# Sinkhorn attention into a hypermixer: another written order, mask products ahead of the first loads, projection weights loaded in fp32

## The chip, the cores and the metric

The kernel runs on one core of a Trainium2 chip. The metric is device time in microseconds of one execution; the median of three runs is shown, and one further execution was recorded by the hardware profiler. The engines are PE (TensorE, the matrix products), ACT (ScalarE), DVE (VectorE), POOL (GpSimd) and SP (SyncE, here a DMA queue). In this kernel PE's results go to PSUM, which it uses as one tile of eight banks of 512 fp32 values per partition, and ACT and DVE copy them out. The trace shows each engine taking its instructions in the written order.

## The reference

Four batches, eight heads, 768 positions, head size 64, eight blocks of 96 positions. A Sinkhorn matrix P of 8 x 8 per head sorts the blocks of k and v; each block of q attends to its sorted block; the eight heads laid side by side (512 columns) then go through a token mixer and an output projection.

```python
P = sort_net
for _ in range(5):
    P = P - np.max(P, axis=-1, keepdims=True)
    P = np.exp(P)
    P = P / (np.sum(P, axis=-1, keepdims=True) + 1e-09)
    P = P / (np.sum(P, axis=-2, keepdims=True) + 1e-09)
k_sorted = np.einsum('bhij,bhjcd->bhicd', P, k_b)
v_sorted = np.einsum('bhij,bhjcd->bhicd', P, v_b)
scores = scale * np.matmul(q_b, k_sb.transpose(0, 1, 2, 4, 3))   # within a block
attn = softmax(scores)
x = np.matmul(attn, v_sb)                  # heads side by side: (4, 768, 512)
wq = x @ w_q;  wk = x @ w_k                # 512 -> 64
W_tok = np.einsum('bsd,btd->bst', wq, wk) / np.sqrt(64)
out = np.maximum(np.einsum('bst,btd->bsd', W_tok, x), 0.0) @ w_out
```

The mixer is computed as wq (wk^T x), so that no 768 x 768 matrix appears.

## The kernel before

The whole program is unrolled, and one string, `ORDER`, gives the order of every unit of work. An item such as `K02:6` is unit K of batch 0, part 2, in PSUM bank 6; capital letters are PE units, small letters the copies that empty the bank, with the engine behind the colon (`k02:D:6`: DVE, bank 6). `l` items are loads, issued on POOL and converting fp32 to bf16 on the way (`lk2` is k of batch 2); R, d and s are DMAs on SP. Since every engine takes its items in this order, an item that waits holds up everything behind it on its engine.

The units, in the order in which a batch needs them:

- a, c: the exponentials (ACT) and the row and column sums (DVE) of the five Sinkhorn rounds, for all 32 heads at once. In `a02` (`u_a`, n = 2) ACT's exponential is followed by eight PE products of the identity that build the mask `m_p`, and by ACT's copy of it. i00 makes the identity `idb` on POOL, i03 sets padding.
- Z: products on a zero tile `fil`, which compute nothing that is used. `Z019` is 19 of them.
- B, u, n: eight PE products spread the matrix (`PbT`, the transposed last result of c05); u copies it to `PTR`; n multiplies it with the mask into `M`, the sorting matrix, two heads at a time on DVE for batch 0, four heads on POOL for the others. M has two buffers.
- Q turns q by transposes, K sorts and turns k in one product with M, V sorts v (b > 0). For batch 0, Y and F sort v by way of a turned copy.
- S, e: scores and ACT's exponential. P, r, x: products with the sorted v, reciprocals and scaling on DVE, to `X`. R brings the sorted v across partitions by DMA, N touches it on POOL.
- T, J, W, G, H: T turns X into `XT`; J gives both projections, `qkT`, from `XT` and the weights `wqk`; d copies its q half to other partitions; W turns the k half back by four 128-column transposes per unit, of which w copies columns 64 to 127 to `wk`; G multiplies wk with X; H mixes and applies the relu.
- O, o, s: the output product of 128 rows by 512 columns in four steps, the copy to `ot`, and the store.

Most PE instructions are recorded at line 147, the helper `mm`, and most copies at lines 151 (ACT) and 153 (DVE), the helper `copy`; groups are told apart by their tiles. The POOL queue, before, runs

```
i00 lq0 i03 lv0 lk0 lq1 n11 lv1 lk1 lq2 n10 n20 lk2 lp n21 lv2 lk3 n31 n30 lq3 lv3 lo N35 N15 N25
```

where `lp` loads the two projection weights and `lo` the output weights. After the last batch POOL checks the reciprocals (lines 442 to 448).

Of the kernel before, what the change touches and what calls it, by code (L numbers as in the profile page):

```python
# [16 lines left out]
ORDER = """
i02:D c00:D a01:A i00:G lq0 Z019:0 Q01:0 Q00:1 c01:D a02:A c02:D a03:A i03:G c03:D a04:A c04:D
Q03:2 a05:A c05:D Z010:3 B00:3 n01:D:3 u00:A:3 lv0 Z02:4 Y01:4 n02:D:3 lk0 n03:D:3 n00:D:3 Y03:6
y01:A:4 lq1 Q02:3 y03:D:6 q01:A:0 Y00:4 y00:A:4 q00:A:1 F01:0 q03:D:2 q02:D:3 Z03:6 K02:6 f01:D:0  # L20
K03:4 Y02:2 k02:D:6 K00:0 K01:6 n11:G lv1 k03:D:4 k01:A:6 y02:D:2 Z01:4 S05:4 e05:A:4 F03:6 k00:D:0
S04:2 S02:4 F02:7 S00:0 f03:D:6 e02:A:4 Q10:6 Q11:4 F00:5 f02:D:7 e04:A:2 e00:A:0 q10:D:6 lk1 S01:2
Q12:6 q11:D:4 f00:D:5 Q13:7 lq2 P03:0 q12:D:6 e01:A:2 n10:G S06:4 e06:A:4 V12:2 q13:D:7 r03:D:0
v12:A:2 V11:6 x03:D:0 S03:4 P04:0 r04:D:0 x04:D:0 v11:A:6 e03:A:4 P00:2 V10:6 K13:0 v10:A:6 r00:D:2
n20:G K10:4 lk2 x00:D:2 k10:A:4 lp K11:2 K12:6 k13:D:0 n21:G k12:D:6 S15:0 P01:4 r01:D:4 k11:A:2
S16:2 e16:A:2 P02:6 S12:2 x01:D:4 e15:A:0 Q21:4 r02:D:6 R14:S R15:S Q20:5 e12:A:2 R13:S R10:S R12:S
x02:D:6 S10:0 S13:2 e10:A:0 q20:D:5 T00:6 T02:7 t02:D:7 e13:A:2 t00:D:6 q21:D:4 S11:0 e11:A:0 T03:5
T01:7 S14:2 e14:A:2 t03:D:5 Q23:6 K20:0 lv2 K21:4 lk3 R11:S k20:A:0 q23:D:6 K23:2 k21:D:4 Q22:6
t01:A:7 K22:0 q22:D:6 n31:G P12:4 k23:A:2 J01:7 k22:A:0 j01:A:7 r12:D:4 x12:D:4 P11:2 J00:6 S20:0
n30:G P10:4 r11:D:2 j00:A:6 S26:6 d01:S e20:A:0 x11:D:2 r10:D:4 W00:2 x10:D:4 e26:A:6 W01:3 lq3  # L30
V22:0 P13:6 w01:A:3 V21:3 w00:D:2 T11:2 r13:D:6 T10:5 v22:A:0 R25:S V20:0 x13:D:6 t10:D:5 v20:D:0
S22:6 v21:A:3 S24:3 t11:D:2 G00:5 d00:S e22:A:6 e24:A:3 G01:5 K32:6 R23:S g00:D:5 P14:0 K31:2 K33:4
k32:A:6 k31:A:2 r14:D:0 T12:6 lv3 x14:D:0 S21:0 T13:7 H02:2 e21:A:0 h02:A:2 k33:D:4 R20:S t12:D:6
H00:4 R24:S K30:0 t13:D:7 Q32:7 R22:S Q31:6 Q33:2 Q30:3 h00:D:4 k30:A:0 q33:D:2 S25:4 S23:0 R21:S
q30:D:3 q32:A:7 e23:A:0 lo q31:D:6 J11:2 J10:3 e25:A:4 S34:6 H01:0 e34:A:6 j11:D:2 V31:4 j10:D:3
P23:2 W10:6 h01:D:0 v31:A:4 r23:D:2 W11:7 w10:D:6 V32:0 w11:A:7 P22:4 x23:D:2 r22:D:4 v32:A:0 d11:S
V30:6 P21:2 v30:A:6 O02:0 O03:1 x22:D:4 P24:4 r21:D:2 P20:6 x21:D:2 o03:A:1 r24:D:4 O00:3 R31:S
T21:1 t21:A:1 G10:2 x24:D:4 o00:A:3 r20:D:6 R34:S o02:D:0 x20:D:6 G11:2 S36:4 S30:0 R30:S s01:S
S32:6 R35:S T20:3 e36:A:4 e30:A:0 O04:4 t20:D:3 g10:D:2 d10:S T22:5 e32:A:6 S33:0 o04:D:4 R33:S
R32:S t22:A:5 S31:2 H10:6 T23:4 h10:D:6 O01:5 t23:D:4 e31:A:2 e33:A:0 O05:2 H12:6 o01:A:5 H11:3  # L40
o05:A:2 h12:D:6 S35:0 s00:S J20:5 j20:A:5 J21:2 P31:6 O14:5 h11:A:3 e35:A:0 r31:D:6 s02:S x31:D:6
j21:A:2 O12:4 o12:A:4 P34:0 P32:6 O11:2 r34:D:0 d21:S O10:4 r32:D:6 o11:A:2 x32:D:6 P30:6 W21:2
o14:A:5 x34:D:0 P33:0 o10:D:4 O15:5 r30:D:6 O13:4 W20:3 w21:A:2 T31:2 x30:D:6 o15:D:5 T30:5 w20:D:3
s10:S r33:D:0 o13:A:4 G20:4 d20:S t30:A:5 x33:D:0 G21:4 T32:3 T33:0 t31:D:2 g20:A:4 H22:6 H21:4
t33:A:0 H20:1 N35:G h21:A:4 h20:A:1 t32:D:3 J30:3 J31:0 j31:A:0 O22:4 s11:S s12:S j30:D:3 d30:D
W30:5 O20:3 W31:0 O23:1 w31:A:0 o23:A:1 w30:D:5 o20:D:3 G30:5 G31:5 h22:D:6 d31:D g30:D:5 N15:G
O21:3 H30:0 N25:G o21:A:3 o22:D:4 s21:S H32:6 O24:5 h30:D:0 O25:4 h32:A:6 o24:A:5 H31:2 s20:S
o25:A:4 O31:7 s22:S h31:D:2 O35:6 O33:2 O30:3 o31:A:7 O34:7 o35:D:6 O32:6 o30:D:3 o33:A:2 s31:S
s35:S s33:S o34:A:7 s30:S s34:S o32:A:6 s32:S
# [4 lines left out]
def kernel(  # L54
# [107 lines left out]
    def u_a(b, n, e, bank):  # L162
        nc.scalar.activation(Pv, Pv, ACT.Exp)  # L163
        if n == 2:
            for j in range(NB):
                mm(PS[:, 7, 0:SP], idb, idb[:, j * SP:(j + 1) * SP], start=(j == 0), stop=(j == NB - 1))
            nc.scalar.copy(m_p, PS[:, 7, 0:SP])
# [483 lines left out]
```

## Time and profile before

| What | Value |
|---|---|
| Median of three runs | 109.87 us (109.6 to 111.01) |
| Profiled execution, its own time | 110.02 us |
| Its span, first to last instruction | 107.8 us |
| Mean granted TensorE clock | 0.984 |
| PE busy | 93.8 us (87%), 1499 matmuls |
| DVE busy | 74.1 us (69%) |
| ACT busy | 65.9 us (61%) |
| POOL busy | 26.5 us (25%) |
| Share of PE in the chain that ended last | 60% |
| Bytes moved by DMA | 19.34 MB, mean 179 GB/s |

The span is what the profile covers; the rest of the execution's own time, 2.2 us, lies around it. Busy shares are means over stages that differ, so the time line and windows of a few microseconds say more than the table. A matmul's recorded duration includes its way through the array, which overlaps the next one's: 35 products on `fil` of 512 columns average 475 ns each in the groups, while warm ones start 216 ns apart. PE's busy share is therefore no measure of how full it is.

### The profile page before, as it was taken

The numbers are of one execution on the slowest core, as the hardware profiler recorded it, in microseconds if no ns is written. First come the engines' busy times: TensorE is split into PE (matmuls) and PEld (weight loads), VectorE is DVE, ScalarE is ACT, GpSimd is POOL, SyncE is SP. The second block draws the span as 40 slices with busy tenths as digits, with TensorE's granted clock in tenths as the row PEclk, the third lists the DMA queues.
The fourth block names the chain that finished last, engine by engine and source line by source line (L and its number), as shares of the span: only waits on it lengthen the run. The fifth ranks groups of instructions, "written<-read, shape, count | busy, mean of one in ns | idle before, by whom it ended". The sixth has DMA issues, their size and how long they took to land.

```text
span 107.8 us, 3505 instructions
## 1 busy us (share of the span) xinstructions
PE 93.8 (87%) x1499; PEld 64.1 (59%) x1499; DVE 74.1 (69%) x146; ACT 65.9 (61%) x95; POOL 26.5 (25%) x45
## 2 busy tenths in 40 slices
PE   5997717989998895998989599999999999999960
PEld 2335315767887784868877378676556685553420
DVE  2630765888979986696977589957756984585420
ACT  4102106527979886987878949289695269347440
POOL 7930006959920990000000000000100047000000
PEclk9999996699999999999999999999999999999999
DMA  0899999999999999999999810375270365009784
GB/s 3 89 200 204 204 203 205 115 199 203 205 206 204 231 235 225 204 204 208 205 231 250 198 29 0 104 249 166 88 299 26 146 228 234 3 3 383 298 324 163
DMA packets 19359, 19.34 MB, mean 179 GB/s; under 512 B 1936, under 2 KB 17424, under 8 KB 19344
## 3 DMA queue, kind: packets, MB, share of 16 engines
q0 software_dynamic: 14064, 10.09, 62.8%
q1 hardware_dynamic: 5280, 9.03, 24.0%
q8 instruction: 11, 0.18, 0.6%
q14 instruction: 4, 0.03, 0.1%
HBM read 20.19 MB, written 6.29 MB: 246 GB/s over the span
## 4 chain that ended last, share of the span: by engine, by line
PE 60%; DMA 12%; ACT 10%; DVE 8%; issue 5%; SPq 1%; POOL 0%; POOLq 0%; ACTq 0%
PE ps L147 60%; DMA Qn<-in_q_dram 7%; DMA qD<-qkT 5%; ACT E L321 5%; ACT Vs L151 3%; DVE KT L153 2%; DVE M L240 1%; DVE X L350 1%; ACT KT L151 1%; DVE tmp L182 1%; ACT Pm L163 1%; DVE Pm L179 1%; DVE tmp L177 1%; DVE tmp L178 1%; DVE tmp L183 1%
## 5 line engine op out<-in xcount | busy, mean ns | idle before, releaser
L321 ACT ACTIVATE E<-ps 96x960 bf16<-96x960 f32 (+1 forms) x28 | 23.7, 898 | 4.2 <-PE ps L147 2.2
L147 PE MATMUL ps<-wo,mixT 128*128 128x512 bf16 x96 | 22.9, 379 | 0.0
L350 DVE TENSOR_TENSOR X<-ps,Rall 96x896 bf16<-96x896 f32 (+1 forms) x20 | 20.0, 1004 | 0.6
L151 ACT COPY ot<-ps 128x512 f32<-128x512 f32 x16 | 9.3, 589 | 9.6 <-PE ps L147 9.5
L147 PEld LDWEIGHTS <-mixT 128*128 128x128 bf16 x96 | 8.6, 97 | 9.0 <-issue 0.6
L147 PE MATMUL ps<-fil 128*128 128x512 bf16 x35 | 11.2, 475 | 1.6 <-DVE fil L195 1.2
L240 POOL TENSOR_TENSOR M<-PTR,m_p 128x512 bf16<-128x512 bf16 x6 | 7.9, 1318 | 16.8 <-ACT PTR L151 10.9
L151 ACT CAST KT<-ps 128x768 bf16<-128x768 f32 x11 | 8.6, 808 | 5.1 <-PE ps L147 4.6
L147 PE MATMUL ps<-VT,E 96*128 96x65 bf16 x256 | 10.8, 193 | 0.0
L412 DVE TENSOR_SCALAR mixT<-ps 128x1024 bf16<-128x1024 f32 x7 | 8.6, 1224 | 3.1 <-PE ps L147 3.1
L147 PEld LDWEIGHTS <-KT 64*128 64x128 bf16 (+1 forms) x288 | 8.6, 98 | 3.5 <-issue 1.9
L147 PEld LDWEIGHTS <-E 96*128 96x128 bf16 x256 | 9.7, 97 | 1.6
L153 DVE CAST KT<-ps 128x768 bf16<-128x768 f32 x9 | 8.3, 953 | 3.0 <-PE ps L147 2.8
L147 PE MATMUL ps<-QT,KT 64*128 64x96 bf16 x256 | 9.3, 204 | 0.2 <-ACT E L321 0.2
L307 POOL COPY gate<-VT 6x1 bf16<-6x1 bf16 x3 | 0.5, 177 | 35.3 <-DMA VT<-Vs 35.2
L147 PE MATMUL ps<-M,Kn 128*64 128x128 bf16 x192 | 7.5, 221 | 1.5 <-ACT E L321 1.1
L147 PE MATMUL ps<-idb,Qn 128*64 128x128 bf16 x192 | 7.4, 226 | 1.1 <-DMA Qn<-in_q_dram 0.8
L151 ACT CAST Vs<-ps 128x1024 bf16<-128x1024 f32 x8 | 7.8, 1014 | 0.2
L147 PEld LDWEIGHTS <-Kn 128*64 128x64 bf16 x192 | 6.0, 109 | 3.0 <-issue 2.8
L147 PEld LDWEIGHTS <-fil 128*128 128x128 bf16 x35 | 3.9, 119 | 6.5 <-issue 3.6
L147 PE MATMUL ps<-XT,wqk 128*128 128x384 bf16 x32 | 6.2, 327 | 1.3 <-issue 1.3
L147 PEld LDWEIGHTS <-Qn 128*64 128x64 bf16 x192 | 6.2, 114 | 1.9 <-DMA Qn<-in_q_dram 1.3
(78 smaller groups left out, 136.5 us busy)
## 6 DMA issues: line engine op xcount, KB each, us to landing
out_dram<-ot SPq DMA_DIRECT2D x9, 512.0 KB, 3.2
...
```

The lines of the kernel that those rows point to most:

```text
L147: nc.tensor.matmul(o, w, x, is_transpose=t, start=start, stop=stop, skip_group_check=True)
L151: nc.scalar.copy(o, i)
L153: nc.vector.tensor_copy(o, i)
L163: nc.scalar.activation(Pv, Pv, ACT.Exp)
L177: nc.vector.reduce_sum(tmp, Pv, axis=AX.X)
L178: nc.vector.reciprocal(tmp, tmp)
L179: nc.vector.tensor_mul(Pv, Pv, rows(tmp))
L182: nc.vector.reduce_sum(tmp, (Pm if n == 1 else Pv).rearrange("p i j -> p j i"), axis=AX.X)
L240: ENG[e].tensor_tensor(out=M[b % 2][:, h0:h0 + hn], in0=src.unsqueeze(2).to_broadcast([P, hn, SP, NB]), in1=m_p.unsqueeze(1).unsqueeze(3). ...
L321: nc.scalar.activation(E[b % 2][:, n, 0:2 * w * BLK].rearrange("p (t a c) -> p a t c", a=2, c=BLK), PS[0:BLK, bank:bank + 2, 0:w * BLK].re ...
L350: nc.vector.tensor_mul(xo.rearrange("p (a t d) -> p a t d", a=2, d=D), avps(bank, w)[:, :, :, 0:D], Rall[:, b, n, :, 0:w].unsqueeze(3).to_ ...
L412: nc.vector.tensor_relu(o, i)
```

## The change

Five things change.

- A new PE unit `A00` holds the eight mask products. It stands first in PE's order; `a02` only copies the result. `lq0` goes ahead of `i00`, and the memsets of `i03` behind `n11`.
- The loads `lp` are gone. SP loads both projection weights at the start, unconverted, four rows (1 KB) per partition, into a part of the output tiles `ot`. Unit z00 casts and interleaves them on ACT, U00 transposes, z01 reorders columns on ACT, U01 transposes back, and z02 writes `wqk` on DVE. (The branch under `SPQ` is off.)
- W takes the k half by products with 64 columns of the identity, in fp32 in PSUM; two units share a bank, and for batches 0 to 2 one copy w empties both.
- For the last batch the output rows 4 and 5 are computed and copied in two halves of 256 columns (`O34` and `O314`, `O35` and `O315`).
- The whole order is another one. Batch 0 sorts k before v. POOL's queue is now

```
lq0 i00 lk0 lv0 lv1 n11 i03 n10 lk1 lq1 n20 lv2 lq2 n21 lq3 lk2 lv3 n30 n31 lk3 N15 lo N25 N35
```

```diff
@@ -13,40 +13,41 @@
 ACT = mybir.ActivationFunctionType
 
 NMIX = 2
+SPQ = False
 
 ORDER = """
-i02:D c00:D a01:A i00:G lq0 Z019:0 Q01:0 Q00:1 c01:D a02:A c02:D a03:A i03:G c03:D a04:A c04:D
-Q03:2 a05:A c05:D Z010:3 B00:3 n01:D:3 u00:A:3 lv0 Z02:4 Y01:4 n02:D:3 lk0 n03:D:3 n00:D:3 Y03:6
-y01:A:4 lq1 Q02:3 y03:D:6 q01:A:0 Y00:4 y00:A:4 q00:A:1 F01:0 q03:D:2 q02:D:3 Z03:6 K02:6 f01:D:0
-K03:4 Y02:2 k02:D:6 K00:0 K01:6 n11:G lv1 k03:D:4 k01:A:6 y02:D:2 Z01:4 S05:4 e05:A:4 F03:6 k00:D:0
-S04:2 S02:4 F02:7 S00:0 f03:D:6 e02:A:4 Q10:6 Q11:4 F00:5 f02:D:7 e04:A:2 e00:A:0 q10:D:6 lk1 S01:2
-Q12:6 q11:D:4 f00:D:5 Q13:7 lq2 P03:0 q12:D:6 e01:A:2 n10:G S06:4 e06:A:4 V12:2 q13:D:7 r03:D:0
...
-O21:3 H30:0 N25:G o21:A:3 o22:D:4 s21:S H32:6 O24:5 h30:D:0 O25:4 h32:A:6 o24:A:5 H31:2 s20:S
-o25:A:4 O31:7 s22:S h31:D:2 O35:6 O33:2 O30:3 o31:A:7 O34:7 o35:D:6 O32:6 o30:D:3 o33:A:2 s31:S
-s35:S s33:S o34:A:7 s30:S s34:S o32:A:6 s32:S
+i02:D c00:D a01:A lq0 i00:G c01:D A00:0 a02:A:0 Z020:0 Q00:0 Q02:1 c02:D a03:A c03:D a04:A c04:D
+z00:A a05:A c05:D q00:A:0 lk0 U00:2 Z09:0 B00:0 n03:D:0 Q01:3 q02:A:1 q01:A:3 n02:D:0 Q03:1 n00:D:0
+z01:A:2 u00:D:0 Z02:4 K00:4 n01:D:0 lv0 k00:A:4 K03:6 K01:2 k01:D:2 q03:A:1 K02:4 lv1 k02:D:4 Z01:0
+S02:0 Y03:2 Y02:4 k03:A:6 n11:G e02:A:0 y02:A:4 Y01:6 y03:D:2 S04:0 e04:A:0 Y00:2 F02:4 y01:D:6
+S05:5 S03:0 i03:G y00:D:2 f02:A:4 n10:G F03:7 e03:A:0 F01:2 S00:3 lk1 V12:0 f03:D:7 F00:7 f01:D:2
+v12:D:0 e05:A:5 e00:A:3 S06:5 f00:D:7 S01:2 P02:0 e06:A:5 e01:A:2 lq1 P04:4 V10:6 K12:2 v10:A:6
+r04:D:4 r02:D:0 x02:D:0 K10:0 x04:D:4 k12:A:2 K11:6 n20:G P03:4 r03:D:4 k11:A:6 P01:2 lv2 V11:6
+k10:A:0 Z01:0 Q13:0 x03:D:4 Q11:1 v11:A:6 r01:D:2 Q10:4 R15:S x01:D:2 R14:S q10:A:4 q11:D:1 P00:5
+q13:D:0 r00:D:5 S12:2 R10:S T01:4 K13:0 e12:A:2 k13:A:0 x00:D:5 Q12:7 S11:2 lq2 U01:5 z02:D:5 n21:G
+R11:S q12:D:7 R13:S V20:0 t01:D:4 T03:6 t03:D:6 lq3 e11:A:2 R12:S v20:A:0 S10:2 S14:4 e10:A:2 S16:0
+e14:A:4 V22:6 T02:2 T00:3 v22:D:6 t02:A:2 P10:4 S15:6 t00:D:3 P11:2 e16:A:0 r10:D:4 x10:D:4 e15:A:6
+r11:D:2 J00:0 lk2 j00:A:0 P13:6 S13:4 x11:D:2 J01:0 Q21:3 r13:D:6 R25:S T10:2 e13:A:4 j01:A:0 lv3
+P14:4 x13:D:6 q21:A:3 r14:D:4 d00:S t10:A:2 n30:G R21:S P12:0 W00:3 V21:6 W01:3 d01:S x14:D:4
+r12:D:0 Q22:2 x12:D:0 Q20:4 v21:A:6 R24:S Q33:5 T11:6 T12:7 n31:G R23:S q20:D:4 q22:A:2 w00:D:3
+T13:4 t11:A:6 q33:D:5 K20:0 K23:2 t13:D:4 K21:5 G00:4 R20:S G01:4 t12:D:7 lk3 Q23:7 k23:A:2 k21:A:5
+R22:S k20:D:0 K22:2 k22:D:2 S21:0 S22:5 g00:A:4 e21:A:0 J10:4 q23:D:7 H00:2 e22:A:5 V31:0 j10:D:4
+h00:D:2 J11:7 v31:A:0 j11:D:7 d11:S V32:4 S26:2 e26:A:2 S23:0 S24:6 e23:A:0 Q32:2 Q31:3 e24:A:6
+v32:D:4 R34:S K31:4 q31:D:3 q32:D:2 K32:0 k31:A:4 K33:6 k32:D:0 H01:2 V30:4 k33:A:6 h01:D:2 P22:0
+W10:6 r22:D:0 v30:A:4 N15:G W11:6 Q30:7 w10:A:6 x22:D:0 S25:2 lo R31:S q30:D:7 e25:A:2 H02:4 O02:6
+P24:0 h02:A:4 R32:S K30:2 r24:D:0 G10:7 k30:A:2 R35:S G11:7 x24:D:0 S20:4 g10:A:7 S34:0 e20:A:4
+R33:S P21:2 d10:S O00:7 P23:4 o02:D:6 r21:D:2 e34:A:0 S32:0 R30:S x21:D:2 S33:2 e32:A:0 o00:D:7
+r23:D:4 O01:6 e33:A:2 T21:7 P20:0 x23:D:4 S36:4 t21:D:7 r20:D:0 S30:2 o01:A:6 e36:A:4 x20:D:0 O03:7
+T23:4 S31:5 o03:D:7 H10:0 T20:7 h10:D:0 e30:A:2 e31:A:5 O05:3 P32:5 P30:0 t20:D:7 T22:7 t23:D:4
+r32:D:5 o05:A:3 r30:D:0 P31:2 O10:4 t22:A:7 x32:D:5 N25:G s01:S x30:D:0 O04:5 S35:6 H12:0 o10:A:4
+r31:D:2 e35:A:6 o04:D:5 J20:4 O11:5 s02:S h12:A:0 x31:D:2 P33:6 o11:D:5 J21:0 j20:D:4 P34:2 O15:1
+o15:A:1 j21:D:0 r33:D:6 W20:0 W21:0 w20:A:0 r34:D:2 T31:4 T30:5 x33:D:6 t31:A:4 O14:1 d21:S t30:A:5
+x34:D:2 T33:0 T32:2 o14:D:1 t32:D:2 H11:6 t33:D:0 G20:5 G21:5 J31:4 d20:S J30:0 s10:S g20:A:5
+h11:D:6 s00:S j31:D:4 d31:D j30:A:0 H20:1 H22:5 H21:3 h20:A:1 h21:D:3 O12:7 W31:0 W30:1 O20:2 O21:3
+O13:4 w31:D:0 h22:A:5 o13:A:4 s12:S o20:A:2 o21:D:3 d30:D O23:0 o12:A:7 w30:D:1 s11:S O22:1 o22:D:1
+G30:2 s20:S G31:2 O25:7 g30:A:2 H31:5 N35:G o23:A:0 O24:0 h31:A:5 H30:3 o24:D:0 H32:1 o25:A:7 O32:5
+h30:A:3 s21:S o32:A:5 O33:0 O31:3 h32:A:1 s22:S s32:S o33:D:0 O30:4 O35:0 o31:A:3 s33:S o30:A:4
+O315:1 s31:S o35:A:0 o315:A:1 O314:4 O34:0 o314:D:4 o34:A:0 s30:S s35:S s34:S
 """
 
 
@@ -107,7 +108,7 @@
 
     NIN = 3
     Qn, Kn, Vn = (tiles(n, NIN, [P, H, R6, D]) for n in ("Qn", "Kn", "Vn"))
-    wqk = sb.tile([P, PT, 2, DH], BF16, name="wqk")
+    wqk = sb.tile([P, PT, 2 * DH], BF16, name="wqk")
     wo = sb.tile([P, PT, DM], BF16, name="wo")
     QT = tiles("QT", 2, [P, NP, R6, P])
     KT = tiles("KT", 2, [P, NP, S + PAD])
@@ -123,6 +124,16 @@
     mixT = tiles("mixT", NMIX, [P, 2, 2, R6, P])
     NOT = 4
     ot = tiles("ot", NOT, [P, 2, DM], FP32)
+    if SPQ:
+
+        q32 = XT[0].rearrange("p t s -> p (t s)").bitcast(FP32).rearrange("p (h r d) -> p h r d", r=R6, d=D)
+        nc.sync.dma_start(out=q32.rearrange("p h r d -> p h (r d)"),
+                          in_=q[0, 0:H // 2].rearrange("h (p r) d -> p h (r d)", p=P))
+
+    w32 = ot[0][:, 0, :].rearrange("p (s x) -> p s x", s=2)
+    w16, wT = (ot[1].rearrange("p a n -> p (a n)").bitcast(BF16)[:, n * DM:(n + 1) * DM] for n in range(2))
+    for s, w in enumerate((moe_w_q, moe_w_k)):
+        nc.sync.dma_start(out=w32[:, s], in_=w.rearrange("(p u) d -> p (u d)", p=P))
     M = tiles("M", 2, [P, H, SP, NB])
     Rall = keep.tile([BLK, B, NG, 2, AG // 2], FP32, name="Rall")
     PTR = sb.tile([P, NB, BH], BF16, name="PTR")
@@ -162,12 +173,14 @@
     def u_a(b, n, e, bank):
         nc.scalar.activation(Pv, Pv, ACT.Exp)
         if n == 2:
-            for j in range(NB):
-                mm(PS[:, 7, 0:SP], idb, idb[:, j * SP:(j + 1) * SP], start=(j == 0), stop=(j == NB - 1))
-            nc.scalar.copy(m_p, PS[:, 7, 0:SP])
+            nc.scalar.copy(m_p, PS[:, bank, 0:SP])
         elif n == 3:
             nc.scalar.copy(Lx.rearrange("p a j s -> p (a j) s"),
                            idb[0:BH, 0:BH].unsqueeze(2).to_broadcast([BH, BH, SP]))
+
+    def u_A(b, n, bank):
+        for j in range(NB):
+            mm(PS[:, bank, 0:SP], idb, idb[:, j * SP:(j + 1) * SP], start=(j == 0), stop=(j == NB - 1))
 
     def u_c(b, n, e, bank):
         if n == 0:
@@ -207,10 +220,7 @@
             nc.gpsimd.memset(Rall[:, :, NG - 1, :, (NU - AG * (NG - 1)) // 2:AG // 2], 1.0)
 
     def u_l(b, n, e, bank):
-        if n == "p":
-            for s, w in enumerate((moe_w_q, moe_w_k)):
-                nc.gpsimd.dma_start(out=wqk[:, :, s, :], in_=w.rearrange("(t p) d -> p t d", p=P))
-        elif n == "o":
+        if n == "o":
             nc.gpsimd.dma_start(out=wo, in_=moe_w_out.rearrange("(t p) d -> p t d", p=P))
         else:
             t, src = {"q": (Qn, q), "k": (Kn, k), "v": (Vn, v)}[n[0]]
@@ -305,6 +315,23 @@
     def u_N(b, n, e, bank):
 
         nc.gpsimd.tensor_copy(gate[0:R6, :], VT[b % 2][0:R6, NB - 1, H - 1, 0:1])
+
+
+
+    def u_U(b, n, bank):
+        for t in range(PT):
+            mm(bf(bank)[:, t * P:(t + 1) * P], (w16, wT)[n][:, t * P:(t + 1) * P], idb, t=True)
+
+    def u_z(b, n, e, bank):
+        if b == 1:
+            copy(e, Qn[0][:, 2 * n:2 * n + 2], q32[:, 2 * n:2 * n + 2])
+        elif n == 0:
+            copy(e, w16.rearrange("p (u s d) -> p s u d", u=PT, s=2),
+                 w32.rearrange("p s (u d) -> p s u d", u=PT))
+        elif n == 1:
+            copy(e, wT.rearrange("x (p u) -> x p u", u=PT), bf(bank)[:, 0:DM].rearrange("x (u p) -> x p u", u=PT))
+        else:
+            copy(e, wqk.rearrange("p t d -> p (t d)"), bf(bank)[:, 0:DM])
 
 
     def u_S(b, n, bank):
@@ -361,7 +388,7 @@
 
     def u_J(b, n, bank):
         for pt in range(PT):
-            mm(PS[:, bank, 0:S // 2], wqk[:, pt].rearrange("p a d -> p (a d)"),
+            mm(PS[:, bank, 0:S // 2], wqk[:, pt, :],
                XT[b % 2][:, pt, n * 384:(n + 1) * 384], start=(pt == 0), stop=(pt == PT - 1))
 
     def u_j(b, n, e, bank):
@@ -375,13 +402,12 @@
             copy(e, o, i)
 
     def u_W(b, n, bank):
-        for ii in range(4):
-            i = 4 * n + ii
-            mm(bf(bank)[0:BLK, ii * P:(ii + 1) * P], qkT[b % 2][:, i * BLK:(i + 1) * BLK], idb, t=True)
+        for i in range(4 * n, 4 * n + 4):
+            mm(PS[0:BLK, bank, i * DH:(i + 1) * DH], qkT[b % 2][:, i * BLK:(i + 1) * BLK], idb[:, DH:P])
 
     def u_w(b, n, e, bank):
-        copy(e, wk[b % 2][:, 4 * n:4 * n + 4, :],
-             bf(bank)[0:BLK, 0:4 * P].rearrange("p (i x) -> p i x", x=P)[:, :, DH:P])
+        i0, i1 = (4 * n, 4 * n + 4) if b == B - 1 else (0, NB)
+        copy(e, wk[b % 2][:, i0:i1, :].rearrange("p i x -> p (i x)"), PS[0:BLK, bank, i0 * DH:i1 * DH])
 
     def u_G(b, n, bank):
         for i in range(4 * n, 4 * n + 4):
@@ -411,16 +437,23 @@
         else:
             nc.vector.tensor_relu(o, i)
 
+    def osplit(b, n):
+
+        r, m = n % 10, n // 10
+        return (r, slice(m * DM // 2, (m + 1) * DM // 2)) if b == B - 1 and r >= R6 - 2 else (r, slice(0, DM))
+
     def u_O(b, n, bank):
+        r, c = osplit(b, n)
         for t in range(PT):
-            mm(PS[:, bank, :], mixT[b % NMIX][:, t // 2, t % 2, n, :], wo[:, t, :],
+            mm(PS[:, bank, c], mixT[b % NMIX][:, t // 2, t % 2, r, :], wo[:, t, c],
                start=(t == 0), stop=(t == PT - 1))
 
     def oslot(b, n):
         return ot[(b * 3 + n // 2) % NOT]
 
     def u_o(b, n, e, bank):
-        copy(e, oslot(b, n)[:, n % 2, :], PS[:, bank, :])
+        r, c = osplit(b, n)
+        copy(e, oslot(b, r)[:, r % 2, c], PS[:, bank, c])
 
     def u_s(b, n, e, bank):
         od = out[b].rearrange("(p r) e -> p r e", r=R6)
```

More of the change, by code (lines that the diff above doesn't have):

```diff
@@ L23 @@
-Q12:6 q11:D:4 f00:D:5 Q13:7 lq2 P03:0 q12:D:6 e01:A:2 n10:G S06:4 e06:A:4 V12:2 q13:D:7 r03:D:0
[L24 to L46, printed above, removed]
```

## The prediction

> **What bounds the kernel now.** I read the page's slices first (PE busy, granted clock, DMA share), then the chain of work that ended last, in order of time, then the list of waits, then busy time by windows.
>
> ```profile
> PE   5997717989998895998989599999999999999960
> PEclk9999996699999999999999999999999999999999
> DMA  0899999999999999999999810375270365009784
> ```
>
> Each column is 2.7 us, counted from 0. PE is full from slice 23 on; DMA is full from slice 2 to 21, the loads of q, k, v. The clock dips in slices 6 and 7.
>
> ```profile
> 1.46 7.53 DMA Qn<-in_q_dram
> ...
> 9.03 1.17 PE ps L147 x32
> 10.19 0.02 issue
> 10.22 0.17 ACT m_p L167
> 10.39 0.16 ACT Pm L163
> ...
> 15.56 0.24 DVE PbT L186
> 15.80 0.04 issue
> 15.84 0.36 PE ps L147 x8
> ...
> 61.62 42.61 PE ps L147 x511
> 104.24 0.02 issue
> 104.26 0.59 ACT ot L151
> ```
>
> ```profile
> ACT m_p L167 <- PE ps L147: 5.3, 1, 5.3
> PE ps L147 <- DVE PbT L186: 2.9, 1, 2.9
> ```
>
> ```profile
> 17.90:25.00 7.10, 6.71 (x126) 5.43 (x125) 5.85 (x9) 3.56 (x6) 5.93 (x7) 0.82 1.18 168
> 65.00:70.00 5.00, 5.00 (x81) 3.57 (x79) 4.76 (x10) 3.00 (x5) 0.00 (x0) 1.00 0.21 55
> ```
>
> The waits give us in total, times and the longest; the windows give their length, the busy time of PE, weight loads, DVE, ACT and POOL, the granted clock, the DMA share and GB/s. Three stages follow. **Front, to 16.7:** five Sinkhorn rounds run between ACT and DVE. The mask products (x8, for m_p) sit on PE behind the first Q turns, and those wait for q, which lands at 8.98. ACT, in order, stands at m_p's copy for 5.3 us, and the third exponential starts at 10.29 in the timeline, though its input was ready at 6.38 (6.17 + 0.21 on DVE). PE then waits 2.9 us for PbT. **Middle, 16.7 to 66.6** (first sorted product Y01 to first output product O02): PE is often without a free PSUM bank; ACT and DVE clear them. **End, 66.6 to 104.24:** PE has a backlog; the chain is 42.6 us of nothing but PE.
>
> **Prices.** In the timeline a group of PE instructions lasts its back-to-back time plus about 0.16 for the last one's own way through. Less that, a unit costs: Q, K, Y 0.35 (24 in 0.86), V 0.45 (8 in 0.61), F 0.49, S 0.22 (10 in 0.39), P 0.44 (14 in 0.60), T 0.35, J 0.65, W 0.23 (4 in 0.39), G 0.45, H 0.22, O 0.864 (24 in 5.35 is 6 units). Copies come from the groups by form: E 0.97, KT 0.81 on ACT and 0.95 on DVE, Vs 1.01 and 1.21, QT and XT 0.80 and 0.55, X 1.08, Rall 0.24, mixT 1.03 and 1.22, ot 0.59 and 0.68. I add these along both order lists.
>
> **Front, part by part.** Mask products first: they need idb, now made after the first q issue (0.62 + 1.14, then 0.5), at 2.3 rather than 1.3. They are done by 2.8; m_p is wanted after a02's exponential at 4.9. So the third exponential goes to 6.4, 3.9 us earlier, and PbT from 15.80 to 11.85. What is late next is PE's queue ahead of B00: 20 fillers from 2.8, two Q units, U00, 9 fillers. Before, the clock rose 5.5 us after the first filler (0.43 each until 6.75, 0.216 after); with the same delay 13 cold and 7 warm fillers end at 9.8, Q and U at 10.7, nine more at 12.6. PbT then stands 0.75 (bounds 0 and 1.6, by when the clock rises). B00 costs 0.35, and K00 wants the third of three M products on DVE, 0.44 each: K00 at 14.3. Y01 began at 16.71. The front gives 2.4, not 3.9, but with Q01 and Q03 already ahead of it.
>
> Weights: two 128 KB loads go on SP behind Pm's issue (0.40; nothing else is on SP until 31.8), in the ramp where slice 1 moves only 89 GB/s. Wanted at 8.4 by z00, they land near 4. z00 (512 elements, about 0.6) fits into ACT's 1.5 us of idle between two exponentials; if the loads come after 8.4, the delay goes whole into Sinkhorn. U is 8 transposes, 0.46: U00 lies before B00 in time that was idle, U01 with z02 (0.4 on DVE) is counted below. Removed: the two converting weight loads. They landed at 40.1 and 41.1 after k2's 39.1, so they held the stream 2.0 us for 0.13 MB.
>
> The trace shows SP's and POOL's transfers sharing one DMA share that never exceeds about 204 GB/s while q, k, v load; 256 KB is 1.3 us of that. The Trainium skill, "DMA: Bandwidth & Descriptors", section "Issuing engines are not separate DMA queues", says transfers of all issuers run on the same 16 engines and interleave. By that rule the weight loads are not free: k0 would land 1.3 later, at about 13; by the ramp row they cost nearly nothing. K00 at 14.3 covers both.
>
> **Middle.** Along the lists, from Y01 to O02 before: PE 36.1, ACT 42.7, DVE 43.3 in 49.9 us, so the two that clear PSUM are 86% busy and PE 72%. From K00 to O02 after: PE 33.5, ACT 41.1, DVE 40.0; three Q units and their copies have gone ahead, two P, two S and a K behind O02. At 86%, (41.1 + 40.0) / 2 / 0.861 = 47.1 and O02 starts at 61.4; at PE's ratio, 33.5 x 1.38 = 46.3 and 60.6. I take 61.2, nearer the busier engines. The clock dip (0.82 in 17.9 to 25) is worth at most 7.1 x 0.18 = 1.3; PE would come warm out of the fillers, but was not the bound there: zero taken, 1.3 kept for the low end.
>
> W by 64 columns: no row has this form. Bounds: 57 ns a product as now, or 31 as for the 65-column P products ((0.60 - 0.19) / 13). I take 31, the nearest width: 0.1 a unit, 0.8 in all, 0.4 of it in the end stage. The Trainium skill, "TensorE: Matmul & The Clock Gate", section "Wait — 56ns, not 53.3ns?", gives about 62 ns per matmul for the sequencer when it decodes in software; by that W would gain nothing and the total would be 0.4 higher. The 31 ns of P disagrees with it here. The w copies merge for three batches: 0.37 + 0.28 becomes one of about 0.65, nothing.
>
> **Loads.** Landing is issue plus time to landing in the DMA issues: v0 12.8, k0 16.6, q1 20.5, v1 25.7, k1 30.2, q2 33.9, k2 39.1, v2 45.3, k3 49.6, q3 53.7, v3 59.1, wo 62.9; 3.85 us apart, more where POOL's n11 held up lv1 (5.2) and where VT writes interleave. After: q0 issues at 0.62 instead of 1.46, so q0 8.5, k0 12.5, v0 16.4, v1 20.2. Then POOL waits for PTR (14.7), n11 1.3, the moved memsets 1.04, n10 1.3: lk1 at 18.4, plus v1's 7.3, so k1 at 25.7: the dip stays. Then q1 29.9, v2 33.8, q2 39, q3 43, k2 47, v3 51, k3 56, wo 60. Uses, at 1.40 us per us of PE work from K00: V20 33.6, K20 47.2, K31 56.7, O02 61.2. Each load arrives within 1.2 us of its use: the front's gain has nearly used up the 3 to 5 us of slack that before had.
>
> **End.** 37.6 us for 35.6 of priced PE work, a factor of 1.054. After O02 now 36.9 (what moved behind it, less 0.4 of W): 38.9. PE ends at 100.1 instead of 104.24: 4.1. Halving the last two rows costs eight products of 256 for four of 512, nothing; the last copy falls from 0.59 to about 0.37 (256 elements, the PTR and wk rows): 0.2. What lies behind (2.95 to the span's end) stays. 107.8 - 4.1 - 0.2 = 103.5, plus the 2.2 that the profiled execution has around its span (110.02): 105.7. The median shown is 0.15 below that execution: **105.6**.
>
> **Rivals.** (1) The stream of loads binds: if wo lands at 62.9 as now, O02 starts there, PE ends at 101.8, time 107.3; with v2 or k3 another us late 108.3. For: 99% DMA share and the thin margins; against: 2.0 us less of weight loads and an earlier start. 0.20. (2) Slower: POOL starves the stream. n20 waits until PE has read all of M for batch 0 (Y00), and lv2, lq2, lq3, lk2, lv3 queue behind it. I expect n20 at 21 to 22. v2 needs 7.3 from issue, so beyond 33.8 - 7.3 - 1.3 = 25.2 each us goes whole into V20, K31 and wo; to be slower than 109.87 it must come after about 30; by over 2%, after 32: 112. Against: Y00 comes about 2.5 us of PE work after K00. 0.08. (3) The change does not do what it says: m_p is free, but w16 or the fillers hold PbT's products back, the front gives nothing and the middle order is merely another one: 109.5. Against: each piece has a row with room. 0.08. (4) Better: the warm clock counts, the fillers end before PbT, DVE's lighter load shows: 1.3 + 0.75 more, 103.6. 0.19. The forecast itself, 104.4 to 107: 0.45.
>
> Two per cent, about what a measurement of this kernel can tell (its three runs span 1.3%), is 2.2 us: faster is below 107.7. Forecast, better, and 60% of rival 1: 0.76; slower, rival 2's and 3's far ends: 0.08; the rest 0.16. The range takes in all of the better case and most of rival 1: 103.0 to 109.0.
>
> **What would show it.** m_p's wait on PE gone, PbT near 11.9, PE's first M,Kn products near 14.3, no clock dip in slices 5 to 8, O02 (first wo,mixT row) near 61.2, W's groups of 4 in about 0.3, last ot copies near 0.37. I am wrong if PE waits on Vn, Kn or wo by name, if POOL idles long before an M product, or if fetch stalls (one PE "issue" gap of 1.32 at 60.30 now) have multiplied.

## The result: 118.36 us, 1.072 times the kernel before

| What | Before | After |
|---|---|---|
| Median of the runs | 109.75 us (109.6 to 111.01) | 118.36 us (117.22 to 119.62) |
| Ratio, with its 95% interval | | 1.0723 (1.0599 to 1.0847) |
| Profiled execution, its own time | 110.02 us | 119.62 us |
| Its span | 107.8 us | 117.4 us |
| Start of the first output product (O02) | 66.6 | 70.65 |
| End of the last copy | 104.85 | 113.14 |

The change is slower, and the forecast, 105.6 with a range to 109.0, missed it on the wrong side. The profiled execution is 1.3 us above the median; the accounts below are made against it, and the sums of runs against medians.

The slices of the changed kernel (2.9 us each):

```profile
PE   0499998987497799959579108999999999999930
PEclk9999999999959999999999985599999999999999
DMA  2999999699999999999941893000404192048871
```

The dip of the clock that stood in slices 6 and 7 is gone, as forecast, but slice 11 has one in its place. The DMA share has a hole in slice 7, while nine loads are still to come; PE is nearly empty in slices 22 and 23 (1, 0); and right behind that the clock is at half. The chain of work that ended last, in order of time (start, length, what):

```profile
...
4.84 0.06 ACT m_p L176
4.90 0.04 issue
4.94 6.55 PE ps L158 x32
...
50.20 6.76 DMA VT<-Vs
56.95 5.93 issue
62.89 0.18 POOL gate L317
63.07 0.25 issue
63.31 0.02 POOLq L317
63.33 7.27 DMA wo<-in_moe_w_out_dram
70.60 0.05 issue
70.65 0.61 PE ps L158
```

The front of the chain passes through ACT's copy of the mask to the fillers that wait for it. Its middle goes through a small POOL copy, `gate` (one value in each of six partitions), to the load of the output weights, and O02 starts 0.05 us after that load has landed. The list of waits names the same places (us in total, times, longest):

```profile
POOL gate L317 <- issue: 24.1, 1, 24.1
...
PE ps L158 <- DMA wo<-in_moe_w_out_dram: 5.5, 1, 5.5
...
PE ps L158 <- DMA Kn<-in_k_dram: 2.6, 3, 1.5
PE ps L158 <- DMA Vn<-in_v_dram: 2.3, 2, 1.3
PE ps L158 <- ACT m_p L176: 1.5, 1, 1.5
```

POOL's own time line around the copy (start, duration, instruction, idle time before it) shows what stood in the queue:

```profile
37.88 0.94 POOL L229 DMA_DIRECT2D Kn<-in_k_dram  x1
62.89 0.18 POOL L317 COPY gate<-VT 6x1 bf16<-6x1 bf16 x1 [24.06 <-issue]
63.33 0.75 POOL L224 DMA_DIRECT2D wo<-in_moe_w_out_dram  x1 [0.26 <-issue]
```

k3 is issued at 37.88, then POOL stands for 24 us, and only then comes `lo`. The standing instruction is N15, which reads `VT` of batch 1. VT has two buffers, and in the written order N15 comes after R34, batch 3's first write into the same buffer. So N15 waits not for batch 1's data but for R34's. SP issues that DMA first of the five in this line of its time line:

```profile
60.46 6.83 SPq L312 DMA_DIRECT2D VT<-Vs  x5
```

In the trace it lands 2.29 us later, at 62.75, and N15 runs at 62.89. The list calls the releaser "issue"; the landing time and the written order say what it was.

That gives three suspects, in the order of their size: the gate ahead of `lo`, the hole in the loads, and the fillers that wait for the mask copy.

### The profile page after: what moved, and what is told of

Read it like the earlier page. It is cut to its first block, busy times and chain, and to the rows that moved or that the text cites. A ratio compares the mean times of both kernels' runs of the same rounds, so it can differ in the third digit from the quotient of the medians.

```text
span 117.4 us, 3545 instructions
## 1 busy us (share of the span) xinstructions
PE 93.7 (80%) x1504; PEld 65.2 (56%) x1513; DVE 72.3 (62%) x142; ACT 71.1 (61%) x101; POOL 24.9 (21%) x43
## 4 chain that ended last, share of the span: by engine, by line
PE 49%; DMA 26%; issue 7%; POOL 6%; DVE 3%; ACT 3%; SPq 1%; POOLq 0%; DVEq 0%
PE ps L158 49%; DMA Vn<-in_v_dram 13%; DMA wo<-in_moe_w_out_dram 6%; DMA VT<-Vs 6%; POOL M L250 3%; DMA Pm<-in_sort_net_dram 1%; SPq L312 1%; DVE M L250 1%; ACT Vs L162 1%; ACT E L348 1%; POOL Kn L229 1%; POOL Qn L229 1%; ACT QT L162 1%; DVE XT L164 0%; ACT Pm L174 0%
## 5 line engine op out<-in xcount | busy, mean ns | idle before, releaser
L158 PE MATMUL ps<-wo,mixT 128*128 128x512 bf16 (+1 forms) x97 | 23.1, 370 | 6.1 <-DMA wo<-in_moe_w_out_dram 5.5
L158 PEld LDWEIGHTS <-mixT 128*128 128x128 bf16 x104 | 9.3, 99 | 14.7 <-DMA wo<-in_moe_w_out_dram 5.8
L162 ACT CAST KT<-ps 128x768 bf16<-128x768 f32 x12 | 9.3, 802 | 9.7 <-PE ps L158 9.6
L164 DVE COPY ot<-ps 128x512 f32<-128x512 f32 (+1 forms) x11 | 7.3, 665 | 10.3 <-PE ps L158 7.6
L162 ACT COPY ot<-ps 128x512 f32<-128x512 f32 (+2 forms) x16 | 8.4, 547 | 6.7 <-PE ps L158 6.6
L372 DVE RECIPROCAL Rall<-ps 96x14 f32<-96x14 f32 (+1 forms) x20 | 4.2, 221 | 11.7 <-PE ps L158 9.1
L158 PE MATMUL ps<-fil 128*128 128x512 bf16 x31 | 9.1, 441 | 1.9 <-ACT m_p L176 1.5
L162 ACT COPY QT<-ps 128x768 bf16<-128x768 bf16 x7 | 5.5, 802 | 6.7 <-PE ps L158 3.6
L164 DVE CAST KT<-ps 128x768 bf16<-128x768 f32 x8 | 7.5, 955 | 3.2 <-PE ps L158 3.1
L162 ACT CAST Vs<-ps 128x1024 bf16<-128x1024 f32 x6 | 6.1, 1013 | 3.0 <-PE ps L158 2.7
## 6 DMA issues: line engine op xcount, KB each, us to landing
Qn<-in_q_dram POOLq DMA_DIRECT2D x4, 768.0 KB, 14.7
```

The costliest lines, as they stand in the source:

```text
L158: nc.tensor.matmul(o, w, x, is_transpose=t, start=start, stop=stop, skip_group_check=True)
L162: nc.scalar.copy(o, i)
L164: nc.vector.tensor_copy(o, i)
L372: nc.vector.reciprocal(Rall[:, b, n, :, 0:w], avps(bank, w)[:, :, :, D])
```

## The experiments

### The gate, taken out and put in

a1: the gate copy goes behind `lo`.

```diff
-W10:6 r22:D:0 v30:A:4 N15:G W11:6 Q30:7 w10:A:6 x22:D:0 S25:2 lo R31:S q30:D:7 e25:A:2 H02:4 O02:6
+W10:6 r22:D:0 v30:A:4 W11:6 Q30:7 w10:A:6 x22:D:0 S25:2 lo N15:G R31:S q30:D:7 e25:A:2 H02:4 O02:6
```

> The changed kernel with the POOL item N15 moved from ahead of the output-weight load lo to right behind it, nothing else. Theory G (gate): N15 reads VT's second buffer and stands, in program order, behind the write R34 of batch 3 into the same buffer, so POOL holds lo until R34 has landed (62.89 in the changed kernel). Then lo goes out near 39, wo lands near 64 to 65 behind k3, PE's 5.5 us wait at 65.1 and the half clock after it (about 3 us) go: 118.4 - 8.5 = about 110 us. Theory L (the stream of loads alone is late): wo waits its turn in the stream whatever POOL does, under 2 us gained, 117 us.

Measured: 112.25 us, ratio 1.0216 (1.0123 to 1.0309); O02 at 67.0.

a2: the gate copy keeps its place ahead of `lo`, but goes ahead of R34, so that it no longer waits for R34's data.

```diff
-v32:D:4 R34:S K31:4 q31:D:3 ...
+v32:D:4 N15:G R34:S K31:4 q31:D:3 ...
...
-... v30:A:4 N15:G W11:6 ...
+... v30:A:4 W11:6 ...
```

> The changed kernel with N15 still ahead of lo in POOL's queue, but ahead of R34 in program order, so that it can wait only for batch 1's writes, which landed long before. Theory G: same as with N15 behind lo, about 110 us. If any small POOL instruction ahead of lo does the harm, whatever it waits for: stays at 118 us.

Measured: 111.33 us, ratio 1.0147 (1.0073 to 1.0222); O02 at 66.0. The same stretch of POOL's time line:

```profile
39.11 0.94 POOL L229 DMA_DIRECT2D Kn<-in_k_dram  x1
40.05 0.18 POOL L317 COPY gate<-VT 6x1 bf16<-6x1 bf16 x1
40.17 0.75 POOL L224 DMA_DIRECT2D wo<-in_moe_w_out_dram  x1
```

The gate costs its 0.18 us and nothing else; `wo` lands 24.4 us after its issue, at 64.6, ahead of its use, and PE's list has no wait for it. The span goes from 117.4 to 110.3.

a3: the same mistake in the kernel before: there too R34 and N15 go ahead of `lo`, in that order, and `lo` moves down to where both can stand.

```diff
-q30:D:3 q32:A:7 e23:A:0 lo q31:D:6 ...
+q30:D:3 q32:A:7 e23:A:0 q31:D:6 ...
-... v32:A:0 d11:S
+... v32:A:0 d11:S R34:S N15:G lo
```

> The kernel before with the fault alone put in: R34 first of batch 3's writes, N15 behind it, lo behind N15 (program order R34, N15, lo, all ahead of O02). Theory G: lo waits until R34 lands, some 66 to 69 us, wo lands 7.3 us later at 73 to 76 instead of 62.9, PE stands 7 to 9 us at O02 and loses 2 to 3 us of clock: 118 to 121 us. If the loss of the changed kernel came from its order as a whole and PE has other work to do meanwhile: under 112 us.

Measured: 121.97 us, ratio 1.1117 (1.1035 to 1.1199). The chain:

```profile
66.27 2.29 DMA VT<-Vs
68.56 0.06 issue
68.62 0.18 POOL gate L307
68.80 0.05 issue
68.85 7.85 DMA wo<-in_moe_w_out_dram
76.70 0.05 issue
76.75 39.41 PE ps L147 x416
```

Here the releaser has its name, R34's write, and the rest is the same: the load leaves once the gate has run, PE waits 10.2 us, and the whole backlog of products stands behind it. The mechanism is shown from both sides. `lo` also has a later place in the written order of this kernel, but in POOL's queue only N15 has come between `lv3` and it, and N15 ran 0.06 us after R34's write had landed.

### The fillers and the stream of loads

c1 is a2 with the first fillers in a bank of their own. In the change they share bank 0 with the mask products, and they cannot write there until ACT has copied the mask out.

```diff
-... A00:0 a02:A:0 Z020:0 Q00:0 ...
+... A00:0 a02:A:0 Z020:7 Q00:0 ...
```

> The changed kernel with N15 ahead of R34 (as in a2, 111.3 us) and its 20 fillers in bank 7 instead of bank 0, which they share with the mask products. Theory B (bank): the fillers wait at 3.4 to 4.9 for ACT's copy of the mask out of bank 0; freed, they start 1.6 us earlier, and B00 and K00 1.6 us earlier: 109.7 us. Rival: the loads set the pace after the front (PE waits 6.2 us in all on Q, K and V by name), and a front that is earlier only waits longer: 111 us.

Measured: 109.94 us, ratio 0.9941 (0.9893 to 0.999). PE's first fillers in the changed kernel and, in the second fence, in c1 (start, duration, instruction):

```profile
4.94 0.59 PE L158 MATMUL ps<-fil 128*128 128x512 bf16 x1 [1.49 <-ACT m_p L176]
```

```profile
3.31 2.29 PE L158 MATMUL ps<-fil 128*128 128x512 bf16 x5
```

The wait of 1.5 us is gone; B00, the first product of the spread matrix, starts at 13.0 instead of 15.4 in a2, and O02 at 63.8 instead of 66.0.

c2 is a2 with k1 and q1 issued straight behind v1, ahead of POOL's two products for M and the moved memsets.

```diff
-... K02:4 lv1 k02:D:4 ...
+... K02:4 lv1 lk1 lq1 k02:D:4 ...
```

> As a2, with the loads lk1 and lq1 moved ahead of n11 in POOL's queue (right behind lv1), fillers as in the changed kernel. Theory D (dry stream): in a2 slices 7 and 8 move only 25 and 93 GB/s because lk1 stands behind n11, the memsets and n10; that is about 4 us of loads lost, and PE waits 6.2 us on Q, K, V later. With the stream never dry all later loads land 4 us earlier, PE's waits on them go: 107.3 us. Rival: PE's waits are spread and something else is late next (PSUM copies): 109.5 us or more.

Measured: 108.68 us, ratio 0.9852 (0.9765 to 0.9939). The window from 19 to 22 us of a2, and then of c2 (busy time of PE, weight loads, DVE, ACT and POOL, then clock, DMA share and GB/s):

```profile
19.00:22.00 3.00, 2.92 (x73) 2.18 (x73) 2.92 (x4) 2.97 (x5) 3.00 (x10) 1.00 0.32 49
```

```profile
19.00:22.00 3.00, 2.93 (x78) 2.15 (x73) 2.92 (x4) 2.97 (x5) 2.35 (x10) 1.00 1.31 204
```

The hole is filled, O02 moves from 66.0 to 62.9, and no load is left in PE's list of waits. The front is as late as in a2 (B00 at 15.7), so this is the loads alone, together with a dip of the clock that a2 has behind its wait for q1 (34.0 to 37.4) and c2 has not.

c3 has both edits.

> Both: fillers in bank 7, and lk1 and lq1 ahead of n11. Theory B plus D: 105.7 us, which is the time that the prediction gave for the change. If either is covered by the other: 107 us.

Measured: 109.12 us, ratio 0.9845 (0.9701 to 0.9989): c2 and c3 are the same. In c3 B00 starts at 13.3, 2.4 earlier than in c2, and O02 at 62.9 in both. The lead can be followed in PE's time lines by equal groups: the group of 14 P products that starts at 38.49 in c3 starts at 40.06 in c2 (1.6 ahead); the J products of four, at 41.30 and 42.03 (0.7 ahead). Between them c3 has one PE wait without a named cause (1.34 us, 0.50 in c2), and behind it the clock is at half from 42 to 45, as it is not in c2. The lead was spent on such waits and on the clock, and once the loads came in time an earlier front bought nothing in the medians. The one execution of c3 that kept its clock at 1.0 took 107.94, the others, at 0.976 to 0.982, 109.09 to 109.6; c2's four, all at 0.996 or more, took 108.4 to 109.43. So without the dip the front may be worth some 0.7 us, which one execution does not settle. In c1 the earlier front did help: there POOL's chain came earlier with the front, so k1 was issued at 18.60 instead of 21.05, and the window from 19 to 22 us has 119 GB/s instead of 49. That c1's gain came by way of the loads is the reading that fits all three runs.

### The parts, in the old order

a4: the kernel before, with the mask products as a unit of their own, in bank 7, first on PE. Nothing else.

```diff
-i02:D c00:D a01:A i00:G lq0 Z019:0 ... a02:A c02:D ...
+i02:D c00:D a01:A i00:G lq0 A00:7 Z019:0 ... a02:A:7 c02:D ...
...
+    def u_A(b, n, bank):
+        for j in range(NB):
+            mm(PS[:, bank, 0:SP], idb, idb[:, j * SP:(j + 1) * SP], start=(j == 0), stop=(j == NB - 1))
```

> The kernel before with the mask products alone put first on PE (bank 7), order otherwise as before. The prediction's front: third exponential at 6.4 instead of 10.3, PbT near 11.9, B00 behind its ten fillers near 12.9 instead of 15.84, so 2.9 us earlier, n11 and with it lv1 2.9 us earlier and the dip in the loads (1.35 us) gone: 107.0 us. Rival: what follows is bound by the loads (99% DMA share to 59 us) and the front is given back: 109 to 110 us.

Measured: 106.04 us, ratio 0.9642 (0.9539 to 0.9744): faster than both kernels. In its time line:

```profile
11.68 0.23 DVE L188 STREAM_TRANSPOSE PbT<-Pb 32x64 bf16<-32x64 bf16 x1
12.74 0.36 PE L147 MATMUL ps<-PbT,Lx 32*128 32x32 bf16 x8
```

PbT is there at 11.9 instead of 15.8, and B00 at 12.74 instead of 15.84: 3.1 us, of which O02 keeps 2.5 (64.15 for 66.63). The profiled execution took 107.14, 1.1 above the median, and has a dip of the clock (0.982 in the mean; the other three had 0.993 to 1.0), so O02 shows less here than the ratio does.

d1: all parts of the change in the order of the kernel before (mask first; weights by SP; 64-column W products with merged copies; the last two rows halved).

```diff
-... i00:G lq0 Z019:0 ...
+... i00:G lq0 A00:7 Z019:0 ...
-... Q03:2 a05:A c05:D Z010:3 B00:3 ...
+... z00:A Q03:2 U00:5 a05:A z01:A:5 c05:D Z010:3 B00:3 ...
-... y02:D:2 Z01:4 S05:4 ...
+... y02:D:2 U01:4 z02:D:4 Z01:4 S05:4 ...
-... r23:D:2 W11:7 w10:D:6 V32:0 w11:A:7 P22:4 ...
+... r23:D:2 W11:6 w10:D:6 V32:0 P22:4 ...
-... O35:6 O33:2 O30:3 o31:A:7 O34:7 o35:D:6 O32:6 ...
+... O32:6 O33:2 O30:3 o31:A:7 O35:7 o32:D:6 O315:1 O34:6 ...
```

> All the parts of the change in the order of the kernel before: mask products first, weights by SP in fp32 and turned on chip, W by 64 columns with one copy for batches 0 to 2, the last two output products split; POOL's queue as before without lp, N items last. The mask products alone gave 106.0. The weights take 2.0 us out of the stream of loads; W 0.4 and the tail 0.2 at the end: 103.5 to 105.5 us. Rival: the loads are not what a4 waits for, the extra copies on ACT and DVE cost as much as W saves: 106.0 us.

Measured: 109.45 us, ratio 0.994 (0.9901 to 0.9979). With all parts less is left than with the mask alone, so some part, or some parts together, cost. The next three put one part each on a4.

e1: a4 with W by 64 columns, one bank and one copy per unit, as before.

```diff
-        for ii in range(4):
-            i = 4 * n + ii
-            mm(bf(bank)[0:BLK, ii * P:(ii + 1) * P], qkT[b % 2][:, i * BLK:(i + 1) * BLK], idb, t=True)
+        for i in range(4 * n, 4 * n + 4):
+            mm(PS[0:BLK, bank, i * DH:(i + 1) * DH], qkT[b % 2][:, i * BLK:(i + 1) * BLK], idb[:, DH:P])
```

> The kernel before with the mask products first (a4, 106.0 us) and W by 64-column products, two banks and two copies per batch as before. From the changed kernel's trace a W unit of 4 advances 0.18 us (0.34 less 0.16) against 0.23: 0.05 a unit, half of the units in the saturated end: 0.2 us less, 105.8 us. Rival: the fp32 result doubles what the copies read and they hold G up: 106.5 us.

Measured: 105.82 us, ratio 0.9579 (0.9518 to 0.9639). This is the fastest of all kernels here, and beats both of the pair. Its interval overlaps a4's, so what W adds to the mask is not settled. Its slices have no dip of the clock before the last:

```profile
PE   4997979899896948999986899999999999999930
PEclk9999999999999999999999999999999999999996
```

e2: a4 with the projection weights loaded by SP in fp32 and turned on the chip.

```diff
-... K10:4 lk2 x00:D:2 k10:A:4 lp K11:2 ...
+... K10:4 lk2 x00:D:2 k10:A:4 K11:2 ...
-... Q03:2 a05:A c05:D Z010:3 ...
+... z00:A Q03:2 U00:5 a05:A z01:A:5 c05:D Z010:3 ...
-... y02:D:2 Z01:4 S05:4 ...
+... y02:D:2 U01:4 z02:A:4 Z01:4 S05:4 ...
```

> a4 with the projection weights by SP in fp32, turned on chip (U, z), and the load lp gone. If the loads set the pace in the middle, 2.0 us less of them brings wo and with it the first output product (64.2 in a4) up to 2 us forward: 104.0 to 105.5 us. Rival: the weight loads at the start and the two more copies on ACT before the first sorted products cost as much at the front (B00 at 13.5 in d1 against 12.7 in a4): 106 to 107 us.

Measured: 107.65 us, ratio 0.9824 (0.9754 to 0.9894).

e3: a4 with rows 5 and 4 of the last batch in halves.

```diff
-... O35:6 O33:2 O30:3 o31:A:7 O34:7 o35:D:6 O32:6 o30:D:3 o33:A:2 s31:S
-s35:S s33:S o34:A:7 s30:S s34:S o32:A:6 s32:S
+... O32:6 O33:2 O30:3 o31:A:7 O35:7 o32:D:6 O315:1 O34:6 o30:D:3 o33:A:2 s31:S s32:S s33:S O314:0
+o35:A:7 o315:D:1 s30:S s35:S o34:A:6 o314:D:0 s34:S
```

> a4 with output rows 4 and 5 of the last batch moved to the end and split in two halves of 256 columns, as the change does. Last copy 0.37 to 0.43 instead of 0.59: 0.2 us less, 105.8 us. Rival: the tail behind the last copy is longer wherever the split was in (4.3 us in c2, 3.6 in d1, against 2.9 before and in a4), so the stores land later: 106.5 to 107 us.

Measured: 106.48 us, ratio 0.9628 (0.956 to 0.9697): no effect of the halves shows beside a4.

Of the three, only the weights show a cost, 1.8% beside a4, with intervals that just miss each other (0.9744 and 0.9754). In e2 q0 lands at 9.61 instead of 9.31, B00 starts at 13.27 instead of 12.74, and PE waits 0.7 us for z02. In the new order the same part was tried the other way round.

f1: c3 with the weights loaded as before, by POOL, behind `lv2`.

```diff
-z00:A a05:A c05:D q00:A:0 lk0 U00:2 Z09:0 B00:0 ...
+a05:A c05:D q00:A:0 lk0 Z010:0 B00:0 ...
-z01:A:2 u00:D:0 Z02:4 ... P01:2 lv2 V11:6 ... lq2 U01:5 z02:D:5 n21:G
+u00:D:0 Z02:4 ... P01:2 lv2 lp V11:6 ... lq2 n21:G
```

> The changed order with its three faults mended (c3: N15 ahead of R34, fillers in bank 7, lk1 and lq1 ahead of n11; 0.9845 of before), and the weights loaded and converted by POOL again, behind lv2, instead of by SP and turned on chip; one filler more in U00's place. If the on-chip turning costs in the new order what it cost in the old one (0.982 against 0.964): 0.967 of before, 106.5 us. If in this order the 2.0 us of loads that it saves is worth more, because the middle waits for loads (first output product at 62.9 whatever the front does): 0.995 to 1.0, 110 us.

Measured: 108.2 us, ratio 0.9846 (0.9783 to 0.9908), the same as c3. In the new order no difference shows between the two ways for the weights. For the old order the traces show a part of the cost: q0 takes longer to land where SP loads the weights (the numbers are below), and B00 starts 3.4 us after q0's landing in a4, e1 and e3, and 3.7 in e2 and d1, where U00 has come between. The rest stays open. So does d1: by single parts (3.6% from the mask, 0.6 from W, nothing from the halves, 1.8 lost by the weights) about 0.976 would have come out, not 0.994. In d1 ACT stands 3.9 us ahead of its two w copies, one of them merged (1.8 in e1, ahead of four unmerged ones); whether the merged copies are the cause was not tried by itself.

## Why the prediction was wrong, step by step

The profiled execution was forecast at 105.7 and took 119.62: 13.9 more. By the forecast's own marks: O02 at 70.65 instead of 61.2 (9.45), the stretch from there to PE's end 42.1 instead of 38.9 (3.2), the rest to the end of the span 4.65 instead of 3.4 (1.25).

**The step that failed is Loads**, in its last number: "k3 56, wo 60". It let `wo` follow k3 by 4 us, as if nothing stood between them in POOL's queue. The queue had been written out with N15 between `lk3` and `lo`, and N15 was passed over. The row that would have told is the pair R34 and N15 in the order list: same buffer, so N15 runs when R34's DMA has landed. With a1 and a2 the stall is gone. By what stands in POOL's queue `wo` could not be issued before R34's DMA had landed, and its own landing came at 70.60 instead of 60. Beside a2 the changed kernel is 4.65 us late at O02 and loses 2.6 more by its last copy, which is, within 0.2, the 7.1 us that its span is longer; the medians are 7.0 apart. That is half of the 13.9. Of the rest, 3.3 lie between the spans of a2 and c3, the fillers' bank and the hole in the loads, and 3.5 remain in c3: 1.7 at O02, 0.6 from there to the last copy's end and 1.1 behind it. So the gate was not all: a2, without the stall, took 111.33, still above the forecast range. Rival 2 had the right kind of mechanism, POOL holding a load, at the wrong instruction and with a chance of 0.08; n20 itself ran at 21.85, inside the 21 to 22 expected.

**The forecast for the end stage** failed by the same cause. Its work was as priced; but after 5.5 us without work PE began at half clock. The windows of the changed kernel, columns as above:

```profile
65.00:70.00 5.00, 0.15 (x4) 0.00 (x0) 1.02 (x2) 1.85 (x2) 0.00 (x0) 0.97 1.01 171
70.00:75.00 5.00, 4.13 (x37) 2.95 (x40) 1.49 (x3) 0.80 (x1) 0.18 (x1) 0.50 0.32 75
75.00:80.00 5.00, 4.95 (x89) 3.38 (x87) 2.85 (x5) 3.57 (x5) 0.00 (x0) 0.85 0.01 3
```

Half of the 4.35 us from 70.65 to 75 and 0.15 of the next five are 2.9 us of the 3.2. In c3, without the stall, the stretch from O02 to the last copy's end is 39.9, and the forecast had 38.9 and 0.37 for that copy: 0.6 off.

**Loads, the rest of it.** `lk1` was put at 18.4 and came at 20.02, because M's first product on POOL started at 16.45, not at 14.7. The wording "the dip stays" was right, but its length was not followed through: 154 and 68 GB/s in slices 6 and 7, and k1, landed at 27.3 instead of 25.7, put every later load behind: v2 landed at 38.4 (forecast 33.8), although it was issued at 23.11 and rival 2 gave it until 25.2: it took 15.3 us, behind k1 and q1, not 7.3. k3 landed at 61.2 (forecast 56), and K31 began at 61.22 (forecast 56.7). The sentence that the thin margins leave no slack was right, and was not priced: of K31's 4.5 us, 1.7 were already there at K00; the other 2.8 came behind it, where PE waits 6.3 us in all for q, k and v by name. c2, which fills the hole and leaves the front as it is, is worth 3% beside a2. That is the mechanism of rival 1, the stream of loads as the bound.

**Front.** PbT was forecast at 11.85 and was there at 11.86, and m_p's wait was gone: the mechanism was right, and a4 shows it alone. But "20 fillers from 2.8" passed over the bank: A00 and Z020 both have bank 0, and the fillers started at 4.94, behind ACT's copy. Q came at 10.95, B00 at 14.40 (forecast 12.6), so that PbT stood 2.5 us, beyond the bound of 1.6, and K00 at 16.02 (forecast 14.3). The identity, too, was late: q's issue began at 1.27 instead of 0.62, and the mask products at 3.07 instead of 2.3. Nor was the delay of 5.5 us until the clock rises a constant: from the first filler it was 3.3 us here, and 2.8 to 5.7 over all profiles.

**Weights.** The loads landed 2.1 us after their issue, at 3.3 to 3.8 (forecast about 4), and z00 ran at 8.27 for 0.60 (about 0.6). No cost in this order shows in f1 beside c3, whose interval is 1.4% to either side. For the other loads, though, these two were not nearly free, as the ramp row had it: q0 took 8.83 us from issue to landing instead of 7.52, 1.31 more, as much as the prediction's other price for them (1.3). Over all profiles q0 took 7.35 to 7.85 us in the six without SP's weight loads and 7.55 to 9.09 in the eight with them. Two readings behind these prices were wrong. The rate does pass 204 GB/s while q, k and v load: slices 13 to 15 of the kernel before have 231, 235 and 225. And the removed loads held the stream for 2.0 us only there; in a3, a4, e1, e3 and f1 the second landed 0.7 to 1.5 us after the load ahead of both.

**W.** A unit takes 0.34 us instead of 0.39, which less 0.16 is 45 ns a product: neither the 31 ns taken nor the 57 of the old form. W's products and the copies of the changed kernel, in its groups by form (busy time and mean ns of one, then idle time before them):

```profile
L158 PE MATMUL ps<-idb,qkT 128*96 128x64 bf16 x32 | 2.2, 207 | 0.0
...
L162 ACT CAST wk<-ps 96x512 bf16<-96x512 f32 x2 | 1.2, 584 | 0.0
...
L164 DVE CAST wk<-ps 96x512 bf16<-96x512 f32 x1 | 0.7, 677 | 0.0
```

Merged copies of 0.58 and 0.68 us were forecast at about 0.65. The rival rule, in the Trainium skill, "TensorE: Matmul & The Clock Gate", section "Wait — 56ns, not 53.3ns?", gives about 62 ns a matmul when the sequencer decodes in software; these products did not show it.

**The halves** were forecast to take 0.37 for the last copy, and it took 0.37. Behind it, though, not 2.95 us follow but 4.3: the 256 KB stores took 3.2 us to land, 2.0 in the kernel before. c3 and f1 have 3.1 and 2.9, e1, in the old order and without halves, 3.2, and a4 2.0. The halves are not the cause then. The trace's packets point to another: a 16 KB packet of instructions (queue q8) lies among the last stores in the twelve profiles whose 256 KB stores take 2.5 to 3.5 us to land, and not in the kernel before and a4, where they take 2.0. In the changed kernel it ran from 110.10 for 1.38 us. The two go together in all fourteen profiles, but no run moved that packet, so the cause is not shown.

**The order itself.** The forecast counted on the middle, 41.1 and 40.0 us of ACT and DVE work for 42.7 and 43.3. In c3 K00 began at 14.9 and O02 at 62.9, 48.0 for a forecast 46.9. Beside a4, which has the old order, c3 has O02 at 62.9 instead of 64.2, but 39.9 us instead of 38.1 from there to the last copy, since more work is behind O02, and 4.1 instead of 2.95 behind that. Beside e1, whose profile has no dip (O02 at 62.6), it is not ahead in the middle either. The only part whose gain is shown is the mask, in the old order. With the same parts in both orders, the mended new order has 0.9845 (c3) and the old one 0.994 (d1), with intervals that overlap: a gain of the order is not shown. f1's interval (from 0.9783) lies above that of the mask alone in the old order (to 0.9744).

The sign named in advance did come: PE waits on Vn, Kn and wo by name. The waits of PE without a named cause did not multiply (0.4 us in all, against 2.1 before).
